# A DiT-like block on one core: V gathered per pair of tiles in five copies, attention weights transposed by DMA, rows of a pair permuted

## The chip, the core and the metric

The kernel runs on one core of a Trainium2 chip. Such a core has five engines with their own instruction streams: TensorE (PE; its weight loads are listed apart, as PEld), VectorE (DVE), ScalarE (ACT), GpSimd (POOL) and SyncE (SP). Sixteen DMA engines move data; SP and ACT issue the transfers. The engines wait for each other by semaphores only. The metric is the device time of one execution, in microseconds. A profile is one execution, recorded; its durations are given in us or ns.

## The reference

One block with adaptive layer norms: x is 2048 tokens by 512, the attention has 32 heads of 16 and looks at 8 earlier tokens with a step of 2, the FFN has width 1792.

```python
mod = (_silu(c) @ w_mod).reshape(c.shape[0], 6, 1, -1)
sa, ca, ga, sb, cb, gb = ...
h = _layernorm(x) * (1 + ca) + sa
x = x + ga * _A_ref(h, A_wqkv, A_wo)
h = _layernorm(x) * (1 + cb) + sb
x = x + gb * _B_ref(h, B_w1, B_w3, B_w2)
# _A_ref: 32 heads, Dh = 16, W = 8, dil = 2
idx = pos[:, None] - off[None, :]            # off = 0, 2, ... 14; masked where idx < 0
logits = einsum('bhsd,bhswd->bhsw', q, k[idx]) * Dh ** -0.5
o = einsum('bhsw,bhswd->bhsd', softmax(logits), v[idx])   # then @ wo
# _B_ref: (silu(h @ w1) * (h @ w3)) @ w2
```

## The kernel before, in words

The 2048 tokens are 16 tiles T of 128. Work is recorded as operations, each with its engine, and emitted in the fixed list `ORDER`; `SLOTS` says which buffer or PSUM bank each value takes. So each engine's order is written out, and an engine that waits for one operation holds up all that stand behind it. Waits are worked out from the data and the buffers.

Loads: x comes in six copies (`load_x`, L412), then `w_mod` in parts, wqkv, and the other weights, all issued by SP in the order of the list; only c is issued by ACT. All loads of SP share one queue.

Modulation: PE multiplies `w_mod` by the activated c (L504, L487 for scale and shift; L531 for the two gates ga and gb, whose weights are the buffers `sb_wm_g`). The first gate is multiplied into wo (L946), the second into w2 (L952).

LayerNorm 1 (L555 to L576) makes normalised tiles; PE transposes (L636) or DMA transposes of `ln_T` make h with features on partitions; ACT applies scale and shift (L621, L644).

Projections (L691, L711): q and k with features on partitions, evicted by ACT (L700, L701) into q buffers and into one kT for all tokens; v with tokens on partitions, evicted by ACT (L721) into one of three V buffers and stored to a scratch tensor in DRAM.

Attention, for a pair of tiles at a time: DVE multiplies q by the 8 shifted k (L742, one instruction of 4096 columns per tile). PE sums over each head's 16 features (L752): 16 matmuls per tile, each with 32 output partitions, four of which run side by side in four column groups q. A group's 32 tokens lie in the columns, so logits stand as heads x tokens. DVE and ACT make the softmax (L764 to L797). PE transposes the weights (L807) and ACT evicts them (L811) into `sb_al`. For each tile four copies from the V scratch bring the 8 shifted V rows of 32 tokens each (`values`, L816): on a partition stand 2 neighbouring tokens of one offset, 2048 bytes. DVE multiplies V by the weights in place (L827, 4096 columns), PE sums over the 8 offsets (L855, by `ind2`), ACT evicts (L861), a DMA transposes the result (`sb_ot`), PE multiplies by wo (L867), and DVE adds to x and sums the row (L871).

FFN, in groups of two or four tiles: LayerNorm 2 (L586 to L601), transposes, then for each of 14 slices of F two groups of four matmuls (L883), silu on ACT (L889), product on DVE (L892); then w2 (L921, L909), the last addition on DVE (L931) and the store by SP. FFN matmuls of earlier groups are interleaved with the attention of later pairs.

Of the kernel before, what the change touches and what calls it, by code (L numbers as in the profile page):

```python
# [10 lines left out]
P = 128  # L11
# [62 lines left out]
class Program:  # L74
# [41 lines left out]
    def dma(self, out, in_, key, packets, r=(), w=(), part=(), after=(), eng="sp", cost=450, group=None, transpose=False,  # L116
            store=False, again=False, lat=None):
# [11 lines left out]
        o = self.op(eng, fn, cost, key, r=r, w=w, part=part, after=after, dma=(each, ns, *(lat if lat else (900, 200) if store else (900, 500) if transpose else (1300, 600))))  # L129
        if group is not None:  # L130
            group.append(o)
            o.group = group
        return o
# [115 lines left out]
C_PQ, C_RED, C_ACC = 2203, 455, 800  # L249
# [3 lines left out]
def c_mm(n):  # L253
    return n * 5 // 12 + 3

# [13 lines left out]
AC_OLD = ()  # L269
# [3 lines left out]
def _build(p, A_x, A_wqkv, A_wo, B_w1, B_w3, B_w2, c, w_mod, out):  # L273
# [4 lines left out]
    x_view = x2d.rearrange("(t p) d -> p t d", p=P)  # L278
# [11 lines left out]
    qb = [sb([P, KT, 512], bf, f"q{i}") for i in range(4)]  # L290
# [3 lines left out]
    vshb = [sb([P, 8, D], bf, f"vsh{i}") for i in range(2)]  # L294
    pqb = [sb([P, W, KT, P], bf, f"pq{i}") for i in range(2)]
    NSM = 3
    atb = [sb([P, 2, 32, W], bf, f"attn{i}") for i in range(NSM)]
    alb = [sb([P, 2, 8, H], bf, f"al{i}") for i in range(3)]
    mxb = [sb([P, 2, 32], f32, f"mx{i}") for i in range(NSM)]
    ssb = [sb([P, 2, 32], f32, f"ssum{i}") for i in range(NSM)]  # L300
    otb = [sb([P, KT, P], bf, f"ot{i}") for i in range(3)]
# [5 lines left out]
    ones = sb([P, 256], bf, "ones")  # L307
    ind = sb([P, 16], bf, "ind")
    ind2 = sb([P, 2, 32], bf, "ind2")
    before = sb([P, W, 2, 16], bf, "before")  # L310
# [26 lines left out]
    osb = [nc.alloc_sbuf_tensor_at(f"sb_o{i}", [P, D], bf, offset=nc.lookup_mloc(wqkv).addr + 8192 + 1024 * i) for i in range(4)]  # L337
    vsh_x = nc.alloc_sbuf_tensor_at("sb_vshx", [P, 8, D], bf, offset=nc.lookup_mloc(wqkv).addr)
# [12 lines left out]
    vshpool = Pool("vsh", vshb)  # L351
    pqpool = Pool("pq", pqb)
# [8 lines left out]
    def held(pool, items):  # L361

        vals = []
        for i, item in enumerate(items):
# [5 lines left out]
    qkv_hold = held(vshpool, [vsh_x]) + held(opool, osb)  # L370

    vind2 = Val("ind2")
# [16 lines left out]
                                           pattern=[[-W, 16]], channel_multiplier=1), 200, k, w=[vind])  # L389
    p.op("pool", lambda e: e.affine_select(out=ind[:], in_=ind[:], compare_op=ALU.is_ge, fill=0.0, base=W - 1,  # L390
                                           pattern=[[W, 16]], channel_multiplier=-1), 200, k, w=[vind])
    p.op("dve", lambda e: e.memset(ind2[:], 0.0), 80, k, w=[vind2])
    for y in range(2):
        p.op("dve", lambda e, y=y: e.tensor_copy(bass.AP(ind2, 33 * y, [[64, P], [2, 16]]), ind[:]), 150, k, r=[vind], w=[vind2])
    p.op("pool", lambda e: e.memset(before[:], 0.0), 250, k, w=[vbefore])
    p.op("pool", lambda e: e.affine_select(out=before[:], in_=before[:], compare_op=ALU.is_ge, fill=BEFORE, base=0,
                                           pattern=[[-DIL, W], [1, 2], [2, 16]], channel_multiplier=0), 400, k, w=[vbefore])
# [14 lines left out]
    def load_x(a, b, i):  # L412
        p.dma(x_sb[:, a:b, :], x_view[:, a:b, :], ("load", i), (128 * (b - a), 1024), w=vx[a:b])
# [99 lines left out]
    def warm(i, after=()):  # L513
# [3 lines left out]
        def mm(e):  # L517
            return e.matmul(bank(vw)[:, 0:256], ones[:, 0:P], ones[:], start=True, stop=True)
# [156 lines left out]
    def proj_qk(gi, Ts, kind, vh):  # L675
# [7 lines left out]
        for f0 in range(0, KT, m):  # L683
# [13 lines left out]
            def ev(e, f0=f0, vp=vp):  # L697
                src = bank(vp)[:, 0:m * n].rearrange("p (j n) -> p j n", j=m)
                if kind == 0:
                    return e.activation(dstv.at[:, f0:f0 + m, at0:at0 + n], src, ACT.Copy, scale=SCALE)  # L700
                return e.activation(kT[:, f0:f0 + m, PAD + 512 * cch + at0:PAD + 512 * cch + at0 + n], src, ACT.Copy)  # L701
# [3 lines left out]
    def proj_v(T, tt, vh):  # L705
# [19 lines left out]
        p.dma(v_dram[PAD + T * P:PAD + (T + 1) * P, :], lambda: vt.at[:], k, (128, 1024), r=[vt], w=[vd], cost=400, store=True)  # L725
# [5 lines left out]
    def logits(Ts):  # L731

        vl = Val("ps_l", psum)
        for i, T in enumerate(Ts):
# [11 lines left out]
            def red(e, i=i, T=T, vp=vp):  # L746
                c0 = vl.at * 512 + i * W * 32
                if T == 0:
                    e.matmul(PALL[0:32, c0:c0 + W * 32], ones[:, 0:32], before[:], start=True, stop=False, tile_position=(0, 0))
                for ft in range(KT):  # L750
                    for q in range(4):
                        ins = e.matmul(PALL[32 * q:32 * q + 32, c0:c0 + W * 32], E_sb[:, ft, :], bass.AP(vp.at, ft * P + 32 * q, [[W * KT * P, P], [KT * P, W], [1, 2], [2, 16]]),  # L752
                                       start=(ft == 0 and (T > 0 or q > 0)), stop=(ft == KT - 1), tile_position=(0, 32 * q))
# [3 lines left out]
        return vl  # L757

    def shift(Ts, vl):
# [4 lines left out]
        o = p.op("dve", lambda e: e.tensor_reduce(ve.at[1][:, 0:n], bass.AP(PALL, bank(vl).offset, [[8 * 512, P], [W * 32, n], [1, 32], [32, W]]),  # L764
                                                  AX.X, ALU.max), 66 + 267 * n, k, r=[vl], w=[vm], hold=[ve], lock=False)

        def sub(e):
            l = bank(vl)[:, 0:n * W * 32].rearrange("p (n w t) -> p n w t", n=n, w=W)
            return e.tensor_tensor(l, l, bass.AP(ve.at[1], 0, [[64, P], [32, n], [0, W], [1, 32]]), ALU.subtract)
# [5 lines left out]
    def exps(groups, vls, ves):  # L775
# [3 lines left out]
        def ex(e):  # L779
            for Ts, vl in zip(groups, vls):  # L780
                l = bank(vl)[:, 0:len(Ts) * W * 32]
                ins = e.activation(l, l, ACT.Exp)
# [6 lines left out]
    def softmax(Ts, vl, ve, vx_):  # L789
# [4 lines left out]
        o = p.op("dve", lambda e: e.tensor_reduce(ve.at[2][:, 0:n], bass.AP(PALL, bank(vl).offset, [[8 * 512, P], [W * 32, n], [1, 32], [32, W]]),  # L794
                                                  AX.X, ALU.add), 66 + 267 * n, k, r=[vx_], w=[vs], hold=[ve, vl], lock=False)
        o = p.op("dve", lambda e: e.reciprocal(ve.at[2][:, 0:n], ve.at[2][:, 0:n]), 20 + 225 * n, k, r=[vs], w=[vr], hold=[ve, vl], lead=o, lock=False)
        p.op("dve", lambda e: e.tensor_tensor(ve.at[0][:, 0:n], bass.AP(PALL, bank(vl).offset, [[8 * 512, P], [W * 32, n], [1, 32], [32, W]]),  # L797
                                              bass.AP(ve.at[2], 0, [[64, P], [32, n], [1, 32], [0, W]]), ALU.mult),
             74 + 267 * n, k, r=[vr, vx_], w=[va], hold=[ve, vl], lead=o, lock=False)
        vt, val = Val("ps_at", psum), Val("al", alpool)  # L800

        def turn(e):
            b = bank(vt).bitcast(bf)
            for i in range(n):
                at = b[:, i * 256:(i + 1) * 256].rearrange("p (q y h) -> p q y h", q=4, y=2)
                for y in range(2):
                    ins = e.transpose(at[:, :, y, :], bass.AP(ve.at[0], i * W * 32 + y * 16 * W, [[2 * W * 32, P], [1, P]]), ident[:])  # L807
# [3 lines left out]
        p.op("act", lambda e: e.activation(val.at[:, 0:n].rearrange("p n g h -> p (n g h)"), bank(vt).bitcast(bf)[:, 0:2 * n * P], ACT.Copy),  # L811
# [3 lines left out]
    def values(T, i, val):  # L815

        vv = Val("vsh", vshpool)
        loads = []
        for q in range(4):
            p.dma(lambda q=q: vv.at[:, 2 * q:2 * q + 2, :],  # L820
                  bass.AP(v_dram, (PAD + T * P + 32 * q) * D, [[2 * D, 16], [-DIL * D, W], [1, 2 * D]]), ("vl", T), (128, 2048),
                  r=[vv_dram[T]] + ([vv_dram[T - 1]] if T else [vvpad]), part=[vv], group=loads, cost=640, again=True)

        def av(e):
            a_w = bass.AP(val.at, i * 8 * H, [[2 * 8 * H, P], [H, 8], [0, DH], [1, H]])
            v_w = bass.AP(vv.at, 0, [[8 * D, P], [D, 8], [H, DH], [1, H]])
            return e.tensor_tensor(v_w, v_w, a_w, ALU.mult)  # L827

        avs[T] = p.op("dve", av, C_PQ, ("av", T), r=[val], w=[vv], lock=True)
        vo = Val("ps_o", psum)  # L830

        vt = Val("ot", otpool)
        if T in AC_OLD:
            def acc(e):
                b = bank(vo)
                for g in range(8):
                    for ft in range(KT):
# [238 lines left out]
```

## Time and profile before

| what | value |
|---|---|
| median of 3 runs | 243.87 us (242.85 to 245.49) |
| profiled execution, own time | 242.82 us |
| its span in the profile | 241.1 us |
| granted PE clock | 1.00 throughout |
| DMA moved | 38.85 MB, mean 161 GB/s |
| V gathers | 64 copies of 256 KB, 4.3 to 4.6 us from issue to landing |
| V stores | 16 copies of 128 KB, 5.9 us |
| output stores | 14 of 128 KB, 1.9 us; 4 of 64 KB, 1.5 us |
| DMA transposes | 20 for h (3.9 us), 16 for `sb_ot` (3.3 us) |

How to read the page: busy time of each engine with its share of the span; then DMA queues; then the chain of work that ended last, followed back from the last instruction; then groups of instructions, as "line engine operation out<-in xcount". Busy PE time counts the modelled end of pipelined matmuls, so the number of columns says more about PE's work than its busy time: in the chain, 27 matmuls of 512 columns take 5.99 us. Busy shares of the DMA engines can be over 100%, where an engine has two packets under way. The profile's slices of 6 us show how work is spread (busy tenths; DMA the mean of its 16 engines):

```profile
PE   7988999979999999999799999999999999999995
DVE  5697999979989999898999999764565044423542
ACT  2296497688999744955964578646537253140300
DMA  6999999999979996693893882253220300000103
```

### The profile page before, as it was taken

What the parts mean: (1) busy time and instruction counts of PE and PEld (TensorE: products, weight loads), DVE (VectorE), ACT (ScalarE), POOL (GpSimd) and SP (SyncE); (2) the same over time, 40 slices, a digit from 0 to 9 for tenths busy, and PEclk for the clock granted to TensorE, in tenths of its full rate; (3) what the DMA queues carried; (4) which work ended last, traced back from release to release, by engine and by line L of the source; (5) the groups of instructions that cost most, each with busy time, mean ns of one, the idle gap of its engine ahead of it and who ended that gap; (6) DMA issues with size and microseconds to landing.
All of it is one profiled execution on the core that took longest, in us unless ns stands there. A gap on an engine that the chain in (4) does not pass through costs nothing.

```text
span 241.1 us, 4538 instructions
## 1 busy us (share of the span) xinstructions
PE 230.4 (96%) x1781; PEld 136.8 (57%) x1806; DVE 179.6 (75%) x279; ACT 138.7 (58%) x267; POOL 30.9 (13%) x66
## 2 busy tenths in 40 slices
PE   7988999979999999999799999999999999999995
PEld 4856454544587685564345444444565584485874
DVE  5697999979989999898999999764565044423542
ACT  2296497688999744955964578646537253140300
POOL 4332060004001000250005301001001000000000
PEclk9999999999999999999999999999999999999999
DMA  6999999999979996693893882253220300000103
GB/s 222 370 327 327 163 262 234 287 282 343 331 134 253 283 270 115 160 272 99 213 256 119 195 197 46 66 141 98 76 79 0 46 0 0 3 22 0 48 0 109
DMA packets 46317, 38.85 MB, mean 161 GB/s; under 512 B 21704, under 2 KB 37080, under 8 KB 46296
## 3 DMA queue, kind: packets, MB, share of 16 engines
q1 hardware_dynamic: 46288, 38.56, 62.5%
q8 instruction: 14, 0.23, 0.4%
q14 instruction: 7, 0.06, 0.1%
q10 hardware_dynamic: 8, 0.00, 0.0%
HBM read 29.62 MB, written 4.21 MB: 140 GB/s over the span
## 4 chain that ended last, share of the span: by engine, by line
PE 50%; ACT 1%; DMA 1%; issue 1%; DVE 0%; SPq 0%
PE pall L883 30%; PE pall L921 12%; PE pall L867 3%; PE pall L909 3%; DMA sb_h<-sb_xn 1%; ACT sb_h L621 1%; PE pall L855 1%; PE pall L752 1%; PE pall L807 0%; ACT sb_al L811 0%; DVE sb_o L931 0%; SPq L124 0%
## 5 line engine op out<-in xcount | busy, mean ns | idle before, releaser
L883 PE MATMUL pall<-sb_h,sb_w 128*128 128x256 bf16 (+1 forms) x665 | 101.8, 307 | 1.0 <-ACT sb_h L621 0.6
L883 PEld LDWEIGHTS pall<-sb_h,sb_w 128*128 128x128 bf16 x672 | 64.8, 98 | 36.2 <-issue 1.5
L892 DVE TENSOR_TENSOR sb_hh<-sb_sg,pall 128x256 bf16<-128x256 bf16 (+1 forms) x84 | 40.4, 505 | 32.1 <-PE pall L883 32.0
L889 ACT ACTIVATE sb_sg<-pall 128x256 bf16<-128x256 f32 (+1 forms) x84 | 36.2, 455 | 43.4 <-PE pall L883 37.3
L921 PE MATMUL pall<-sb_w,sb_hh 128*128 128x512 bf16 x189 | 43.7, 379 | 0.4
L742 DVE TENSOR_TENSOR sb_pq<-sb_q,sb_kT 128x4096 bf16<-128x4096 bf16 x16 | 36.3, 2282 | 0.0
L921 PEld LDWEIGHTS pall<-sb_w,sb_hh 128*128 128x128 bf16 x196 | 19.1, 98 | 21.0
L691 PE MATMUL pall<-sb_h,sb_wqkv 128*128 128x512 bf16 (+1 forms) x159 | 30.3, 336 | 0.1
L827 DVE TENSOR_TENSOR sb_vsh<-sb_vsh,sb_al 128x4096 bf16<-128x4096 bf16 x12 | 27.3, 2286 | 2.4 <-ACT sb_al L811 2.2
L621 ACT ACTIVATE sb_h<-sb_h,sb_modc 128x512 bf16<-128x512 bf16 (+1 forms) x24 | 16.3, 733 | 13.0 <-DMA sb_h<-sb_xn 13.0
L691 PEld LDWEIGHTS pall<-sb_h,sb_wqkv 128*128 128x128 bf16 x160 | 15.1, 98 | 12.2 <-ACT sb_h L644 0.5
L931 DVE TENSOR_TENSOR sb_o<-pall,sb_x 128x512 bf16<-128x512 f32 (+1 forms) x18 | 10.9, 627 | 11.8 <-PE pall L921 8.7
L586 POOL TENSOR_SCALAR sb_nm<-sb_sx 128x2 f32<-128x2 f32 x8 | 3.7, 465 | 115.9 <-DVE sb_x L871 115.9
L590 ACT ACTIVATE sb_xn<-sb_x,sb_nm 128x512 bf16<-128x512 bf16 x16 | 11.4, 714 | 11.7 <-POOL sb_nm L586 11.7
L867 PE MATMUL pall<-sb_wo,sb_ot 128*128 128x512 bf16 x60 | 15.0, 379 | 1.1 <-DMA sb_ot<-sb_ac 0.5
L711 PE MATMUL pall<-sb_wqkv,sb_h 128*128 128x512 bf16 x58 | 15.0, 379 | 0.3 <-issue 0.2
L644 ACT ACTIVATE sb_h<-pall,sb_modc 128x256 bf16<-128x256 bf16 (+1 forms) x18 | 9.9, 616 | 8.6 <-DVE sb_modc L509 6.7
L601 ACT ACTIVATE sb_xn<-sb_x,sb_nb,sb_rs 128x512 bf16<-128x512 bf16 x16 | 12.6, 806 | 3.7 <-POOL sb_nb L599 3.7
L871 DVE SCALAR_TENSOR_TENSOR sb_x<-pall,sb_x 128x512 bf16<-128x512 f32 x16 | 11.0, 688 | 2.3 <-PE pall L867 2.3
L701 ACT ACTIVATE sb_kT<-pall 128x512 bf16<-128x512 f32 x16 | 9.6, 606 | 4.7 <-PE pall L691 4.7
L555 DVE BATCH_NORM_STATS2 sb_st<-sb_x 128x6 f32<-128x512 bf16 x16 | 10.4, 678 | 1.3 <-DMA sb_x<-in_A_x_dram 1.3
L721 ACT ACTIVATE sb_v<-pall 128x512 bf16<-128x512 f32 x16 | 9.6, 612 | 2.4 <-DMA v_scratch_dram<-sb_v 2.3
(87 smaller groups left out, 208.6 us busy)
## 6 DMA issues: line engine op xcount, KB each, us to landing
sb_vsh<-v_scratch_dram SPq DMA_DIRECT2D x48, 256.0 KB, 4.6
sb_vshx<-v_scratch_dram SPq DMA_DIRECT2D x16, 256.0 KB, 4.3
sb_w<-in_B_w_dram SPq DMA_DIRECT2D x6, 512.0 KB, 5.6
sb_w<-in_B_w_dram SPq DMA_DIRECT2D x6, 384.0 KB, 6.0
v_scratch_dram<-sb_v SPq DMA_DIRECT2D x16, 128.0 KB, 5.9
out_dram<-sb_o SPq DMA_DIRECT2D x14, 128.0 KB, 1.9
sb_wqkv<-in_A_wqkv_dram SPq DMA_DIRECT2D x6, 256.0 KB, 6.0
sb_x<-in_A_x_dram SPq DMA_DIRECT2D x4, 256.0 KB, 6.3
```

The costliest lines, as they stand in the source:

```text
L590: p.op("act", lambda e, vn=vn, T=T: e.activation(vn.at[:], x_sb[:, T, :], ACT.Square, bias=nm[:, T, :], accum_out=var[:, T, :]), c_act(512 ...
L601: p.op("act", lambda e, vn=vn, T=T: e.activation(vn.at[:], x_sb[:, T, :], ACT.Identity, bias=nb[:, T, :], scale=rs[:, NT + T, :]), c_act(5 ...
L621: return e.activation(vh.at[:, ft, 0:n * P], vh.at[:, ft, 0:n * P], ACT.Identity, bias=modc[:, 8 * which + ft:8 * which + ft + 1], scale=m ...
L691: ins = e.matmul(bank(vp)[:, j * n:(j + 1) * n], wqkv[:, t, col:col + P], vh.at[:, t, 0:n], start=(t == ORDER[0] and j == 0), stop=(t == O ...
L711: ins = e.matmul(bank(vp), vh.at[:, t, tt * P:(tt + 1) * P], wqkv[:, t, 2 * D:3 * D], start=(t == ORDER[0]), stop=(t == ORDER[-1]))
L742: return e.tensor_tensor(vp.at[:], in0, in1, ALU.mult)
L827: return e.tensor_tensor(v_w, v_w, a_w, ALU.mult)
L867: ins = e.matmul(bank(vy), vt.at[:, ft, :], wo[:, ft, :], start=(ft == 0), stop=(ft == KT - 1))
L883: ins = e.matmul(bank(vp)[:, 0:n], wt[:, t, fi * P:(fi + 1) * P], vh.at[:, t, 0:n], start=(t == 0), stop=(t == KT - 1))
L889: p.op("act", lambda e: e.activation(vt.at[:, 0:n], bank(vgp)[:, 0:n], ACT.Silu), c_act(n), k, r=[vgp], w=[vt], table="silu")
L892: p.op("dve", lambda e: e.tensor_tensor(vh_.at[:, 0:n], vt.at[:, 0:n], bank(vup)[:, 0:n], ALU.mult), c_dve(n), k, r=[vt, vup], w=[vh_])
L921: ins = e.matmul(bank(vz), vhh[fi].at[:, tt * P:(tt + 1) * P], w2[:, fi, :], start=(fi == 0), stop=(fi == NF - 1))
```

## The change

What it does:

- **V.** The unit is a pair of tiles, 256 tokens, as 32 blocks of 8 tokens. A partition of the gathered V holds one block and one of 4 offsets (steps of 4 tokens); ten tokens' rows lie on it, brought by 5 copies of 256 KB per pair (before: 4 per tile, 8 per pair). DVE multiplies them in three instructions (6, 2 and 8 rows of 512 columns), partly into a new buffer `sb_av`; PE sums by `ind` (32 columns).
- **Attention weights** are transposed by a DMA issued by SP instead of by PE with an ACT eviction. `AT_PE` is empty, so it is so for all pairs.
- **Rows of a pair are permuted**: tile T's partition p = 32 q + b holds token 8 b + 4 (T mod 2) + q of the pair. x loads, V stores and output stores pick the rows by their DRAM pattern. The q and k evictions write back in the tokens' natural order (a step of 8 elements), and the matmuls that sum over a head's features read with that step.
- **x** is loaded in 16 copies, tile by tile, the second issued by ACT.
- Three q buffers instead of four, two `sb_ot` buffers of a pair instead of three of a tile; six output buffers instead of four.
- `ORDER` and `SLOTS` are new. The gate weights are loaded behind all of x; the second gate's matmuls come first of the two, still ahead of most of the projections.

```diff
+    def rows(t, T, c0=0, n=D):
+        first = T // 2 * 2 * P + T % 2 * 4
+        return bass.AP(t.tensor, t.offset + first * D + c0, [[D, 4], [8 * D, 32], [1, n]])
...
+    def v_rows(T):
+        return bass.AP(v_dram, (PAD + T // 2 * 2 * P + T % 2 * 4) * D, [[D, 4], [8 * D, 32], [1, D]])
...
     def load_x(a, b, i):
-        p.dma(x_sb[:, a:b, :], x_view[:, a:b, :], ("load", i), (128 * (b - a), 1024), w=vx[a:b])
+        for T in range(a, b):
+            p.dma(x_sb[:, T, :], rows(x2d, T), ("load", i if T == a else 40 + T), (128, 1024), w=[vx[T]], eng="act" if T == 1 else "sp")
...
             def ev(e, f0=f0, vp=vp):
-                src = bank(vp)[:, 0:m * n].rearrange("p (j n) -> p j n", j=m)
+                src = bass.AP(PALL, bank(vp).offset, [[8 * 512, P], [256, 2], [32, 8], [1, 32]])
...
+                    out_ = bass.AP(dstv.at, f0 * 512 + at0, [[KT * 512, P], [step_, 2], [1, 8], [8, 32]])
+                    return e.activation(out_, src, ACT.Copy, scale=SCALE)
...
-        p.dma(v_dram[PAD + T * P:PAD + (T + 1) * P, :], lambda: vt.at[:], k, (128, 1024), r=[vt], w=[vd], cost=400, store=True)
+        p.dma(v_rows(T), lambda: vt.at[:], k, (128, 1024), r=[vt], w=[vd], cost=400, store=True)
...
                     for q in range(4):
-                        ins = e.matmul(PALL[32 * q:32 * q + 32, c0:c0 + W * 32], E_sb[:, ft, :], bass.AP(vp.at, ft * P + 32 * q, [[W * KT * P, P], [KT * P, W], [1, 2], [2, 16]]),
-                                       start=(ft == 0 and (T > 0 or q > 0)), stop=(ft == KT - 1), tile_position=(0, 32 * q))
+                        ins = e.matmul(group(q), E_sb[:, ft, :], bass.AP(vp.at, ft * P + q, [[W * KT * P, P], [KT * P, W], [4, 2], [8, 16]]),
+                                       start=(ft == 0), stop=(ft == KT - 1), tile_position=(0, 32 * q))
...
+        if Ts[0] not in AT_PE:
+            p.dma(lambda: val.at[:], lambda: ve.at[0][:], ("at", Ts[0]), (128, 1024), r=[va], w=[val], hold=[ve], cost=1270, transpose=True)
+            return val
...
-        for q in range(4):
-            p.dma(lambda q=q: vv.at[:, 2 * q:2 * q + 2, :],
-                  bass.AP(v_dram, (PAD + T * P + 32 * q) * D, [[2 * D, 16], [-DIL * D, W], [1, 2 * D]]), ("vl", T), (128, 2048),
+        for s in range(5):
+            p.dma(lambda s=s: vv.at[:, 2 * s:2 * s + 2, :],
+                  bass.AP(v_dram, (PAD + T0 * P - DIL + 2 * s) * D, [[8 * D, 32], [-2 * DIL * D, 4], [1, 2 * D]]), ("vl", T0), (128, 2048),
...
+        first = p.op("dve", av(1, 2, 6, 2, vpr, 0), c_av(6), k, r=[val, vin], w=[vhigh], hold=[vv, vpr], lock=True)
+        p.op("dve", av(1, 0, 2, 0, vv, 0), c_av(2), k, r=[val, vin], part=[vlow], hold=[vv], lock=True)
+        o = p.op("dve", av(0, 0, 8, 2, vv, 2), c_av(8), k, r=[val, vin], part=[vlow], hold=[vv, vpr], lock=True)
...
-        finals.append(p.dma(out2d[T * P:(T + 1) * P, c0:c0 + n], lambda: vo.at[:, 0:n], ("zo", T), (128, 2 * n), r=[vo], cost=400, store=True))
+        finals.append(p.dma(rows(out2d, T, c0, n), lambda: vo.at[:, 0:n], ("zo", T), (128, 2 * n), r=[vo], cost=400, store=True))
```

More of the change, by code (lines that the diff above doesn't have):

```diff
@@ L128, in dma @@
         ns = 600 if transpose else each * (126 if again else packet_ns(size))
-        o = self.op(eng, fn, cost, key, r=r, w=w, part=part, after=after, dma=(each, ns, *(lat if lat else (900, 200) if store else (900, 500) if transpose else (1300, 600))))
+        o = self.op(eng, fn, cost, key, r=r, w=w, part=part, after=after, hold=hold, dma=(each, ns, *(lat if lat else (900, 200) if store else (900, 500) if transpose else (1300, 600))))
         if group is not None:
@@ L248 @@
 MM = 216
[L249 removed]
+C_PQ, C_RED = 2203, 455
 BEFORE = -1e9 / P
@@ L863, in values @@
-        vy = Val("ps_y", psum)
-        def wop(e):
-            for ft in range(KT):
-                ins = e.matmul(bank(vy), vt.at[:, ft, :], wo[:, ft, :], start=(ft == 0), stop=(ft == KT - 1))
-            return ins
-        p.op("pe", wop, 4 * MM, ("wo", T), r=[vt, vsc_wo], w=[vy])
-        p.op("dve", lambda e: e.scalar_tensor_tensor(x_sb[:, T, :], bank(vy), 1.0, x_sb[:, T, :], op0=ALU.mult, op1=ALU.add,
-                                                     accum_out=sx[:, T, :]), c_dve(512) + 12, ("rs", T), r=[vy], w=[vx[T], vsx[T]])
+        for s in range(5):
+            p.dma(lambda s=s: vv.at[:, 2 * s:2 * s + 2, :],
+                  bass.AP(v_dram, (PAD + T0 * P - DIL + 2 * s) * D, [[8 * D, 32], [-2 * DIL * D, 4], [1, 2 * D]]), ("vl", T0), (128, 2048),
+                  r=[vv_dram[T] for T in Ts] + ([vv_dram[T0 - 1]] if T0 else [vvpad]), part=[vin], hold=[vv], group=loads, cost=640, again=True)
@@ new lines, in values, with wop @@
+        for n, T in enumerate(Ts):
+            vy = Val("ps_y", psum)
+            def wop(e, n=n, vy=vy):
+                for ft in range(KT):
+                    ins = e.matmul(bank(vy), vt.at[:, ft, n * P:(n + 1) * P], wo[:, ft, :], start=(ft == 0), stop=(ft == KT - 1))
+                return ins
+            p.op("pe", wop, 4 * MM, ("wo", T), r=[vts[n], vsc_wo], w=[vy], hold=[vt])
+            p.op("dve", lambda e, T=T, vy=vy: e.scalar_tensor_tensor(x_sb[:, T, :], bank(vy), 1.0, x_sb[:, T, :], op0=ALU.mult, op1=ALU.add,
+                                                         accum_out=sx[:, T, :]), c_dve(512) + 12, ("rs", T), r=[vy], w=[vx[T], vsx[T]])
```

169 lines of the change are left out of this document (83 added, 86 removed), and 126 rows, old and new, of tables (ORDER, SLOTS).

## The prediction, made before the changed kernel ran

> **What bounds the kernel now.** I read the page first, then the chain that ended last, TensorE's waits, its timeline, and last the DMA traffic in narrow windows. The page's engine and queue rows (engine or queue: busy us, share, instructions; for queues packets, MB, share of 16 engines):
>
> ```profile
> span 241.1 us, 4538 instructions
> PE 230.4 (96%) x1781; PEld 136.8 (57%) x1806; DVE 179.6 (75%) x279; ACT 138.7 (58%) x267; POOL 30.9 (13%) x66
> q1 hardware_dynamic: 46288, 38.56, 62.5%
> q10 hardware_dynamic: 8, 0.00, 0.0%
> ```
>
> TensorE (PE) is the bound, DVE is second, and DMA is far from full over the whole span. The chain in order of time (start, duration, what) says where PE is the bound:
>
> ```profile
> 116.50 5.99 PE pall L883 x27
> ...
> 232.34 6.13 PE pall L909 x56
> 238.47 0.02 issue
> 238.49 0.42 DVE sb_o L931
> ```
>
> From 116.5 us on every piece but waits of some 0.05 us is PE work; then the last eviction, and the last store to 241.1 (2.6 us after PE). Before that, PE waited for data in few places (total, times, longest):
>
> ```profile
> PE pall L531 <- DMA sb_wm_g<-in_w_mod_dram: 1.5, 2, 0.9
> PE pall L752 <- ACT sb_kT L701: 0.9, 1, 0.9
> PE pall L855 <- DVE sb_vsh L827: 0.7, 1, 0.7
> ```
>
> All rows of PE's list of waits sum to about 7 us. The first matters here: the matmuls on the gate weights wait for their load. They stand early in PE's order (timeline: start, duration):
>
> ```profile
> 18.10 0.54 PE L531 MATMUL pall<-sb_csT_bf,sb_wm_g 128*128 128x1 bf16 x16 [0.63 <-DMA sb_wm_g<-in_w_mod_dram]
> ```
>
> Now DMA. In the window 4 to 16 us the 16 engines are full, so a load lands when the bytes ahead of it are through:
>
> ```profile
> DMA packets 3595, 4.42 MB, mean 369 GB/s; under 512 B 191, under 2 KB 2693, under 8 KB 3594
> q1 hardware_dynamic: 3594, 4.41, 107.2%
> ```
>
> That is 369/16 = 23.1 GB/s per engine. How many engines one copy uses can be counted. The window 239.3 to 241.1 holds the last store alone, 128 rows of 512 B:
>
> ```profile
> DMA packets 144, 0.07 MB, mean 36 GB/s; under 512 B 16, under 2 KB 144, under 8 KB 144
> ```
>
> 128 rows make 128 packets, and 16 more are small: one completion from each of 16 engines. The load of c, four rows of 256 B on queue 10, has 8 packets: four rows and four completions, so four engines. By the code, the access patterns of all other copies begin on both sides with a count of 128, 32 or 16, those of c with 4.
>
> **The change, part by part.** Times are against the profiled execution: 242.82 us, span 241.1, so 1.7 us lie around the span; it is 0.4% under the median of 243.87.
>
> 1. *Attention weights by DMA.* Removes 8 groups of 4 PE transposes (L807): 0.22 us each when hidden in the chain, so 8 x 0.22 = -1.8 us on PE, on the path; and 8 ACT evictions (L811, 598 ns) = -4.8 us, off it. The DMA takes the place of at most 2.4 us (the first pair's weights are ready at 36.3, their first user starts at 38.7); the like DMA, sb_ot<-sb_ac, lands in 3.3 us, behind an SP issue of 1.3. In the new DVE order 3.5 to 17 us of other DVE work by its rows stand between the weights and their first user, so DVE waits 0 to 1 us per pair, and the matmuls of L691 and L883 lie beside it. I take 0 on the path, ends 0 and 8.
>
> 2. *V copied 5 instead of 8 times.* 64 copies of 256 KB become 40: -24 x 16 KB per engine = -17 us per DMA engine at 23.1 GB/s, off the path. SP issues 24 fewer at 0.6 us, 8 more transposes at 1.3 and 9 more x loads at 0.45: -14.4 + 10.4 + 4.1, so nothing.
>
> 3. *DVE.* The two products of a pair (2286 ns each) become three over the same 8192 columns. L952 (2048 columns 1219 ns, 1536 columns 950 ns) gives 0.14 us fixed per instruction: 8 x 0.14 = +1.1 us, beside L883 matmuls; 0 on the path. The softmax rows keep their sizes. Two small copies (L394) go, at the start, beside ACT's table load: 0.
>
> 4. *Rows of a pair permuted, inside the chip.* Matmuls of L752 read their moving operand with a step of 8 elements (now 2), and the q and k evictions (L700, L701) write with that step. No row shows such a step. Nearest: L752 itself at full speed (32 in 0.99 us), and L721, which reads PSUM with a step of 16 at 612 ns against 606 without. I take 0; the bounds are no cost, or half speed: 16 tiles x 0.495 us = +7.9 us on PE.
>
> 5. *Start.* A second DMA issue on ACT (0.56 us) now precedes its table load, which leads by way of c to the first LayerNorm: +0.5 us, on the path unless 6 covers it.
>
> 6. *Rows of a pair permuted, in DRAM.* This is the large term. The x loads, the V stores and the output stores now have on the DRAM side the counts 4, 32, 512: they begin with 4. By the count above I take it that such a copy runs on four engines, and that these are the same four each time (the trace cannot show which; the bound if they rotate is a rival). Then in queue order, ahead of the end of the first gate load, each of those four engines has x 2.10 MB / 4 = 524 KB, the modulation weights 1.05 MB / 16 = 66 KB, wqkv 98 KB, the gate load 33 KB: 721 KB / 23.1 = 31.2 us. Bytes begin at about 2.3 us, so it lands at 33.5, with 0.5 us to its completion 34.0, against 18.1 now. In the new PE order the gate matmuls still stand before the transposes of the third LayerNorm group and nearly all else. PE is in order, so what is queued behind them waits: all remaining projections, attention and FFN. That is +15.9 us. Earlier waits are inside it (96 KB more of x stand ahead of wqkv, 4.2 us). Nothing late in the kernel can take it back: PE ran from 18.10 to 238.47 with 4 us of waits.
>
>    V stores: 128 KB / 4 / 23.1 = 1.42 us each on the four engines instead of 0.36: 16 x 1.06 = +17 us of their time, against 12 x 0.71 = -8.5 us for the gathers saved in the first four pairs. Three V buffers stand between ACT and the stores; ACT already waits for a store three times (2.3 us in all). Behind a waiting V eviction on ACT stand the q and k evictions, which hold PSUM banks, so PE waits too. Bounds 0 and 17; I take +5, nearer the difference of the two with half of it hidden.
>
>    Output stores: only the last one is on the path: 64 KB, 16 KB per engine at 23.1 GB/s = 0.7 against 0.2: +0.5 us.
>
> Sum: 242.8 - 1.8 + 15.9 + 5 + 0.5 = 262.4; the 0.5 of part 5 lies inside the 15.9.
>
> [...]
>
> **The rivals.**
>
> *A, four fixed engines:* 262. For: the eight packets of queue 10. Against: those four rows could not have used more than four engines anyway.
>
> *B, faster:* the copies still use 16 engines. Then PE's own wall decides: 242.8 - 1.8 + 0.5 = 241.5, and the new order can at most remove the waits, 5 us: 236.5 to 241.5, so 239.5. For: PE's share of the chain. It decides where an x load shows 16 completions.
>
> *C, as B, but strided reads halve L752:* 239.5 + 7.9 = 247.4. For: the step is new. Against: a step of 2 costs nothing in L752. [...]
>
> *D, four engines that rotate:* no queue grows, each copy takes 1.1 us longer: first x load +1.1, last store +0.5, two waits for V stores +2: 239.5 + 3.6 = 243. The "does little" case.
>
> **How the numbers follow.** Chances: A 0.72, B 0.12, C 0.08, D 0.08. The forecast is A's 262. A's own range: with no cost of V stores and 3.4 us of the remaining waits gone, 254; with 17 instead of 5 for V stores, 274: so 254 to 274. To leave out no more than 2 in 10 the range must take in C and D: 242 to 276 (A inside 0.66, C 0.08, D 0.06, a little of B). About 1% is what a measurement of this kernel can tell from no change: 241.4 to 246.3. Faster by over 1% is B, 0.12; within 1% is D and the fastest edge of A, 0.09; slower is the rest of A, and C, 0.79.
>
> **What would show it.** Right: an x load window with 128 rows and 4 small packets; x loads that land near 20 to 33 us; PE waiting over 10 us for sb_wm_g; the DMA share well under full at 10 to 35 us, with GB/s falling to about a quarter; more ACT waits at the V eviction. Part 1 is right if L807 is gone and DVE waits little for sb_al. C is right if the L752 group's 32 take near 2 us. Wrong: 16 small packets per x load, or a PE wait for the gates under 3 us; then B or C holds. If the four engines rotate, x loads land within 20 us although each has 4 completions.

## The result, and the profile after

| kernel | median, us | ratio to before, 95% interval |
|---|---|---|
| before | 243.8 (242.85 to 245.49) | |
| changed | 315.4 (314.47 to 315.7) | 1.2921 [1.2844, 1.2997] |

The change costs 29%, 71.6 us, far beyond the forecast of 262 and its upper end of 276. Some executions take over 1.5% longer than the fastest of the same kernel; they stay in the medians here and are left out of the ratios. The page of the changed kernel (engines, then queues):

```profile
span 314.0 us, 4468 instructions
PE 265.0 (84%) x1752; PEld 139.7 (44%) x1777; DVE 180.4 (57%) x284; ACT 190.6 (61%) x259; POOL 28.9 (9%) x69
q1 hardware_dynamic: 46612, 33.19, 41.3%
q10 hardware_dynamic: 140, 0.13, 0.1%
```

DMA moves 5.4 MB less on queue 1, as the five V copies should. But PE, at 96% of the span before, is at 84%, and although its matmul work hardly changed it is busy 34.6 us longer. ACT is busy 51.9 us longer with eight instructions fewer. Queue 10 carries c (8 packets) and one x load: 132 packets, which are 128 rows and 4 completions. The slices of the span (here 7.85 us each, busy tenths; PEclk the granted clock) say where:

```profile
PE   6693199756897568998989999999999999999990
ACT  2189858989999997975483662457356543421300
PEclk9997569977799797999999999999999999999997
DMA  6625999760146650792465323532232202100012
```

PE has holes up to 120 us (slice 15) and a last slice with nothing. ACT is full in most of the slices in which PE has holes, and where PE starves its granted clock is lower, too: 5 tenths in slice 5, where PE is busy 1 tenth. The groups (line, engine, operation, tiles, forms, count, then busy us, mean ns, and the idle time before) name the instructions. Before, the q and k evictions and the reduction matmuls were

```profile
L701 ACT ACTIVATE sb_kT<-pall 128x512 bf16<-128x512 f32 x16 | 9.6, 606 | 4.7 <-PE pall L691 4.7
L700 ACT ACTIVATE sb_q<-pall 128x512 bf16<-128x512 f32 x16 | 9.3, 606 | 0.0
L752 PE MATMUL pall<-sb_pq,sb_E 128*32 128x256 bf16 x256 | 9.1, 271 | 0.9 <-ACT sb_kT L701 0.9
```

and in the changed kernel they are

```profile
L714 ACT ACTIVATE sb_q<-pall 128x512 bf16<-128x512 f32 x16 | 40.5, 2596 | 2.7 <-PE pall L703 2.7
L716 ACT ACTIVATE sb_kT<-pall 128x512 bf16<-128x512 f32 x16 | 41.5, 2629 | 0.7 <-PE pall L703 0.6
L770 PE MATMUL pall<-sb_pq,sb_E 128*32 128x256 bf16 x256 | 31.4, 631 | 1.2 <-ACT sb_kT L716 0.8 <-DVE sb_pq L757 0.4
```

An eviction took 606 ns and now takes 2.6 us: +63 us by these rows, whose durations overlap their neighbours' (ACT's busy time grew by 51.9). The 256 reduction matmuls took 9.1 us and now take 31.4: +22 us on PE. Both gained the step of 8 elements. The gate matmuls (timeline: start, duration, and in brackets the wait) start at 37.8 instead of 18.1:

```profile
37.84 0.57 PE L543 MATMUL pall<-sb_csT_bf,sb_wm_g 128*128 128x1 bf16 x16 [7.62 <-DMA sb_wm_g<-in_w_mod_dram]
```

At the end PE's last matmuls (timeline: start, duration) are

```profile
299.56 6.28 PE L926 MATMUL pall<-sb_w,sb_hh 128*128 128x256 bf16 x56
```

They end at 305.8 us, and the last store lands at 314.0: 8.1 us behind PE, where there were 2.6. (The chain that ended last leaves PE earlier, at 301.3 us, since the last evictions wait for output buffers and no longer for PE. So 12.7 us of the chain lie behind it. The texts written ahead of the runs take these 12.7 us for the time behind PE's last instruction.) DMA traffic in the window 308 to 311 us, with only output stores under way:

```profile
DMA packets 339, 0.28 MB, mean 92 GB/s; under 512 B 10, under 2 KB 339, under 8 KB 339
```

92 GB/s is four times the 23.1 GB/s of one engine (369/16 before), and queue 1 takes 27.5% of the 16 engines' time there: by rate and share the stores queue on the same four engines while twelve are empty. The list of waits (total us, times, longest) shows the new ones:

```profile
DVE sb_pq L757 <- ACT sb_q L714: 17.9, 1, 17.9
PE pall L543 <- DMA sb_wm_g<-in_w_mod_dram: 7.8, 2, 7.6
DVE sb_o L948 <- DMA out_dram<-sb_o: 7.6, 4, 4.4
```

So three suspects: the DRAM pattern that begins with 4 (start and tail), ACT's writes with a step of 8 (to SBUF, where the buffers lie; PSUM holds the banks that PE writes), PE's reads with a step of 8. What each is worth, how they overlap, and whether anything is left of the rest of the change, the trace alone can't say.

### The profile page after: what moved, and what is told of

Its sections match the earlier page's. It is cut to its first block, busy times and chain, and to the rows that moved or that the text cites. A ratio compares the mean times of both kernels' runs of the same rounds, so it can differ in the third digit from the quotient of the medians.

```text
span 314.0 us, 4468 instructions
## 1 busy us (share of the span) xinstructions
PE 265.0 (84%) x1752; PEld 139.7 (44%) x1777; DVE 180.4 (57%) x284; ACT 190.6 (61%) x259; POOL 28.9 (9%) x69
## 2 busy tenths in 40 slices
DMA packets 46773, 33.61 MB, mean 107 GB/s; under 512 B 25232, under 2 KB 40608, under 8 KB 46752
## 4 chain that ended last, share of the span: by engine, by line
PE 60%; ACT 20%; SPq 9%; DMA 6%; issue 2%; DVE 0%; ACTq 0%; DVEq 0%
PE pall L900 30%; PE pall L938 13%; SPq L124 9%; ACT sb_q L714 8%; PE pall L770 7%; ACT sb_kT L716 7%; DMA sb_wm_g<-in_w_mod_dram 4%; PE pall L884 4%; ACT sb_h L633 2%; PE pall L871 2%; PE pall L703 2%; PE pall L726 2%; DMA out_dram<-sb_o 1%; DMA sb_ot<-sb_ac 1%; ACT sb_v L736 1%
## 5 line engine op out<-in xcount | busy, mean ns | idle before, releaser
L906 ACT ACTIVATE sb_sg<-pall 128x256 bf16<-128x256 f32 (+1 forms) x84 | 36.4, 463 | 44.7 <-PE pall L900 37.6
L703 PE MATMUL pall<-sb_h,sb_wqkv 128*128 128x512 bf16 (+1 forms) x155 | 36.5, 379 | 12.7 <-ACT sb_q L714 7.4
L714 ACT ACTIVATE sb_q<-pall 128x512 bf16<-128x512 f32 x16 | 40.5, 2596 | 2.7 <-PE pall L703 2.7
L716 ACT ACTIVATE sb_kT<-pall 128x512 bf16<-128x512 f32 x16 | 41.5, 2629 | 0.7 <-PE pall L703 0.6
L770 PE MATMUL pall<-sb_pq,sb_E 128*32 128x256 bf16 x256 | 31.4, 631 | 1.2 <-ACT sb_kT L716 0.8
L938 PEld LDWEIGHTS pall<-sb_w,sb_hh 128*128 128x128 bf16 x196 | 19.1, 98 | 21.4
L851 DVE TENSOR_TENSOR sb_vsh<-sb_vsh,sb_al 128x1024 bf16<-128x1024 bf16 (+1 forms) x16 | 23.3, 1484 | 0.1
L656 ACT ACTIVATE sb_h<-pall,sb_modc 128x256 bf16<-128x256 bf16 (+1 forms) x18 | 10.6, 657 | 14.0 <-DVE sb_modc L521 11.0
L726 PE MATMUL pall<-sb_wqkv,sb_h 128*128 128x512 bf16 x60 | 17.5, 426 | 1.8 <-ACT sb_q L714 0.8
L876 ACT ACTIVATE sb_ac<-pall 128x512 bf16<-128x512 f32 x16 | 9.8, 639 | 15.2 <-PE pall L871 11.9
L598 POOL TENSOR_SCALAR sb_nm<-sb_sx 128x2 f32<-128x2 f32 x8 | 2.4, 298 | 160.6 <-DVE sb_x L888 160.6
```

What stands on the lines that cost most here:

```text
L703: ins = e.matmul(bank(vp)[:, j * n:(j + 1) * n], wqkv[:, t, col:col + P], vh.at[:, t, 0:n], start=(t == ORDER[0] and j == 0), stop=(t == O ...
L714: return e.activation(out_, src, ACT.Copy, scale=SCALE)
L716: return e.activation(out_, src, ACT.Copy)
L726: ins = e.matmul(bank(vp), vh.at[:, t, tt * P:(tt + 1) * P], wqkv[:, t, 2 * D:3 * D], start=(t == ORDER[0]), stop=(t == ORDER[-1]))
L770: ins = e.matmul(group(q), E_sb[:, ft, :], bass.AP(vp.at, ft * P + q, [[W * KT * P, P], [KT * P, W], [4, 2], [8, 16]]), start=(ft == 0), s ...
L906: p.op("act", lambda e: e.activation(vt.at[:, 0:n], bank(vgp)[:, 0:n], ACT.Silu), c_act(n), k, r=[vgp], w=[vt], table="silu")
```

## The experiments

Each suspect was first taken out of the changed kernel alone, then all three together; then each was put back alone; then the disputed costs were measured by themselves. Medians of four or more executions, beside runs of the kernel before on the same chip:

| run | what is in it | median, us | ratio to before, 95% interval |
|---|---|---|---|
| changed | DRAM 4 x 32, writes, reads | 315.4 | 1.2921 [1.2844, 1.2997] |
| e1_rows | writes, reads | 303.92 | 1.2491 [1.2447, 1.2536] |
| e2_evict | DRAM, reads | 286.85 | 1.1806 [1.1773, 1.1838] |
| e3_red | DRAM, writes | 303.35 | 1.2486 [1.2448, 1.2524] |
| e4_all | none of the three | 243.45 | 1.0025 [0.9989, 1.006] |
| f1_dram | DRAM alone | 270.14 | 1.1092 [1.1034, 1.1149] |
| f2_write | writes alone | 290.85 | 1.1968 [1.1924, 1.2013] |
| f3_read | reads alone | 261.57 | 1.0786 [1.0743, 1.083] |

### One suspect out

**e1_rows**: 128 rows side by side in DRAM.

```
-        first = T // 2 * 2 * P + T % 2 * 4
-        return bass.AP(t.tensor, t.offset + first * D + c0, [[D, 4], [8 * D, 32], [1, n]])
+        return bass.AP(t.tensor, t.offset + T * P * D + c0, [[D, P], [1, n]])
...
-        return bass.AP(v_dram, (PAD + T // 2 * 2 * P + T % 2 * 4) * D, [[D, 4], [8 * D, 32], [1, D]])
+        return bass.AP(v_dram, (PAD + T * P) * D, [[D, P], [1, D]])
```

> The changed kernel with one edit: the x loads, the V stores and the output stores take 128 rows that lie next to each other in DRAM (counts 128, 512) instead of 4 x 32 rows (counts 4, 32, 512); the same number of DMAs and bytes. What is computed is then not the reference: tokens meet other tokens' keys. Theory (the four-first pattern puts each of these DMAs on the same four engines): each such DMA shows 16 completion packets, the gate load lands at about 18 us as before instead of 37.8, the work behind PE's last instruction falls from 12.7 us to about 3, and the time falls by 10 us (the tail alone, if ACT's evictions go on bounding the middle) to 26 us (tail and the 15.9 us of the start as forecast): 288 to 304. Rival (the evictions and the reduction matmuls carry all of the loss): 312 to 316.

303.92 us, 11.5 less, at the low end of what was expected. The packet rows of its page:

```profile
DMA packets 47373, 33.61 MB, mean 111 GB/s; under 512 B 25832, under 2 KB 41208, under 8 KB 47352
q10 hardware_dynamic: 152, 0.13, 0.1%
```

Against 46,773 packets in the changed kernel that is 600 more: 50 copies (16 x, 16 V, 18 outputs) with 12 completions more each, so 16 instead of 4. That a completion stands for an engine is an inference. The rates of the changed kernel agree with it: several stores together move 92 GB/s in the tail, and with x loads alone under way (18 to 24 us) DMA moves 96 GB/s at 27.2% of the 16 engines' time, which is what the same four engines would do each time; no run here shows their numbers. About half of the 11.5 us is the tail: 8.1 us behind PE's last matmul became 2.5. Of the start little is left: the gate matmuls begin 12.9 us earlier (24.9 instead of 37.8), but the last k eviction only 6.9 us earlier (132.6 instead of 139.5), as ACT is full between 20 and 120 us with or without late x loads (93.1 and 93.6 of 100 us).

**e2_evict**: the step goes to the PSUM side.

```
-                src = bass.AP(PALL, bank(vp).offset, [[8 * 512, P], [256, 2], [32, 8], [1, 32]])
+                src = bass.AP(PALL, bank(vp).offset, [[8 * 512, P], [256, 2], [1, 32], [32, 8]])
...
-                    out_ = bass.AP(dstv.at, f0 * 512 + at0, [[KT * 512, P], [step_, 2], [1, 8], [8, 32]])
+                    out_ = bass.AP(dstv.at, f0 * 512 + at0, [[KT * 512, P], [step_, 2], [8, 32], [1, 8]])
```

> The changed kernel with one edit: the q and k evictions read PSUM with a step of 32 elements and write 8 tokens side by side, where they read side by side and wrote with a step of 8 elements (16 bytes); same result in SBUF. Theory (the step of the write makes them 2.6 us): L714 and L716 go back to about 0.61 us each, ACT's busy time falls by 63 us to about 128 us, PE's granted clock stays at 1.00 from 60 to 120 us, and the time falls by 15 to 36 us (PE is idle 36 us of 301): 278 to 299. Rival (any step costs the same on either side, in PSUM as in SBUF): L714 and L716 stay above 2 us and the time at 312 to 318.

286.85 us, 28.5 less. The groups of its page:

```profile
L716 ACT ACTIVATE sb_kT<-pall 128x512 bf16<-128x512 f32 x16 | 9.5, 604 | 1.7 <-PE pall L703 1.6
L714 ACT ACTIVATE sb_q<-pall 128x512 bf16<-128x512 f32 x16 | 9.4, 601 | 12.8 <-PE pall L703 12.7
```

The same elements, moved to the same places, at the old price: reading PSUM with a step of 32 elements costs nothing here (604 and 601 ns, where both took 606 before), writing SBUF with a step of 8 costs 2 us (2629 and 2596 ns in the changed kernel). ACT's busy time fell by 55 us, to 135.3, and not by the 63 of the rows that overlap. This edit alone would have saved two fifths of the loss.

**e3_red**: `[4, 2], [8, 16]` plus `q` becomes `[1, 2], [2, 16]` plus `32 * q` in the moving operand of L770.

> The changed kernel with one edit: the reduction matmuls L770 read the products with a step of 2 elements (4 bytes) as in the kernel before, not 8 elements (16 bytes); their PSUM pattern with runs of 16 elements stays. The logits then go to other tokens, so that what is computed is not the reference. Theory (the read's step makes 16 of them 1.9 us): L770 falls from 31.4 us to about 9 us of PE, and the time by up to 22 us, by less where ACT's evictions are what PE waits for: 292 to 312. Rival (the runs of 16 in PSUM, or the four column groups that no longer run side by side for the new output pattern): L770 stays at about 31 us and the time at 314.

303.35 us, 12.1 less, within the theory's range. The group of L770, whose PSUM pattern stayed:

```profile
L770 PE MATMUL pall<-sb_pq,sb_E 128*32 128x256 bf16 x256 | 10.5, 298 | 0.8 <-ACT sb_kT L716 0.8
```

So it is the read's step, not the new runs in PSUM. (The 10.5 instead of 9.1 us come from some of the matmuls: half of them take at most 271 ns, as before, and the slowest 418, in a run whose granted clock was 0.92 on average.)

**e4_all**: the three edits together.

> The three edits together (rows side by side in DRAM, evictions that write 8 tokens side by side, reduction reads with a step of 2): what is left is the rest of the change, V in 5 copies, weights turned by DMA, the new order. What is computed is not the reference, for the same two reasons as in the runs alone. Theory (the three explain the whole loss): 238 to 246, ACT about 128 us, L770 about 9 us. Rival (the new order or the DMA-turned weights cost by themselves): over 250, with DVE or PE waiting for the turned weights or the V copies.

243.45 us, no difference from before that can be measured. The page:

```profile
span 240.9 us, 4493 instructions
PE 230.8 (96%) x1777; PEld 134.6 (56%) x1777; DVE 179.3 (74%) x284; ACT 135.1 (56%) x259; POOL 31.0 (13%) x69
```

The three carry the whole loss, and the rest of the change (V in five copies, weights turned by DMA, the new order) is worth nothing: 5 MB less DMA beside a PE at 96%.

### One suspect in

**f1_dram**, **f2_write** and **f3_read** are e4_all with one of its edits undone.

> The run with all three edits, with the DRAM pattern of four times 32 rows put back: of the three suspected costs only this one is left. The logits go to other tokens (reduction reads with a step of 2), so what is computed is not the reference. Theory (start and tail each cost their own, and nothing hides them): the gate load lands near 38 us, PE is idle some 12 us between 20 and 40 us, 12 to 13 us lie behind PE's last instruction, and the time is 262 to 270, the prediction's own 262 among it. Rival (costs add up as they were when each was taken away alone, 11.5 us for this one): 253 to 257.

270.14 us, +26.7, just above the theory's upper end. Its chain over 27 to 41 us (start, duration, what) holds the gate load:

```profile
26.58 1.25 SPq L124
27.83 0.04 issue
27.87 11.35 DMA sb_wm_g<-in_w_mod_dram
39.22 0.14 issue
39.36 0.57 PE pall L543 x16
```

SP is held at its issues until 27.8 us (12 x loads in a row take it 18.4 us, in e4_all 5.8), and the gate load then takes 11.4 us; that it lies behind what is left of x on the four engines is inferred from the order of the queue. At the end 8.1 us lie behind PE's last matmul (2.5 in e4_all), not the 12 to 13 expected.

> The run with all three edits, with the eviction writes of step 8 put back: only they are left. Rows in DRAM are side by side and the logits go to other tokens, so what is computed is not the reference. Theory (ACT becomes the bound from 20 to 120 us, as L714 and L716 take 2.6 us each): ACT's busy time about 190 us, its slices full from 20 to 110 us, the time 270 to 285. Rival (the writes only hurt because the late x loads had pushed all of ACT's work together): under 260.

290.85 us, +47.4, more than either expected. Busy times between 20 and 120 us (window, length, PE, PEld, DVE, ACT, POOL, granted clock, DMA share, GB/s), f2_write:

```profile
20.00:120.00 100.00, 66.80 (x472) 29.90 (x481) 50.63 (x65) 95.35 (x87) 4.98 (x12) 0.83 0.47 125
```

and e4_all:

```profile
20.00:120.00 100.00, 95.89 (x845) 55.46 (x843) 95.69 (x130) 74.44 (x140) 15.82 (x23) 1.00 0.83 203
```

ACT is full, does 87 instead of 140 instructions, and PE does 472 instead of 845 matmuls in the same time. Of ACT's extra 55 us (190.1 against 135.1), the 25.6 us in which e4_all's ACT is idle here could hide less than half. PE's 66.8 us at a mean clock of 0.83 are, as an estimate, 55 us of work at full speed, 40 us less than in e4_all, and PE has to make that up later: most of the 47.4. The last k eviction begins at 130.0 us instead of 82.2, so the whole loss has arisen by then.

> The run with all three edits, with the reduction reads of step 8 put back: only they are left. Rows in DRAM are side by side and the tokens of a tile meet other tokens' keys, so what is computed is not the reference. Theory (PE is the bound at 96% of the span, so every us of L770 counts): L770 31 us, the time 243.5 + 22 = 262 to 268. Rival (costs add up as they were when each was taken away alone, 12 us for this one): 253 to 257.

261.57 us, +18.1, just below the theory's 262. PE is busy 250.0 us of 259.9, 19.2 us more than in e4_all: where PE is the bound, its dearer matmuls are the loss.

Put in alone, the three cost 26.7 + 47.4 + 18.1 = 92.2 us; together 315.4 - 243.45 = 72.0. DRAM and writes together (e3_red) cost 59.9 instead of 74.1, writes and reads (e1_rows) 60.5 instead of 65.5, DRAM and reads (e2_evict) 43.4, about their sum of 44.8. So 14 of the 20 us of overlap lie between late x and slow ACT, which hold up the same early stretch (late x delays the last k eviction by 22.8 us alone, 105.0 against 82.2, and by 6.9 beside the slow writes), and 5 between ACT and the matmuls that wait for it.

### The costs by themselves

**m1_steps**: e4_all with other steps; the warm-up matmul, for one of six cases:

```
-            return e.matmul(bank(vw)[:, 0:256], ones[:], bass.AP(ones, 0, [[P, P], [0, 2], [1, P]]), start=True, stop=True)
+            if i % 6 == 3:
+                return e.matmul(o, ones[:], bass.AP(ones, 0, [[P, P], [0, 16], [8, 16]]), start=True, stop=True)
```

> The run with all three edits, with steps of other sizes to measure the disputed cost by itself. The 24 warm-up matmuls (full width, 256 columns, about 214 ns, which nothing uses) read with steps of 1, 2, 4, 8, 16 and 32 elements in turn; the reduction matmuls read with a step of 4, PSUM written in runs of two with a step; q is written with a step of 4 elements, k with a step of 2, in orders that send tokens elsewhere (what is computed is not the reference). Theory (the read's rate falls with the step above 4 bytes): warm-up matmuls with steps of 8 and more take 3 to 5 times as long as those with step 1, a step of 4 lies between, and L770 takes 9 to 20 us. Rival (a step alone costs nothing; the four column groups of L770 stopped running side by side): all warm-up matmuls take the same time within 10%. For the writes, theory: a cost that grows with the step: k (step 2, 4 bytes) about 0.6 us, q (step 4, 8 bytes) between 0.6 and 2.6 us.

255.75 us in one execution, which has other steps in three places at once; only its instructions matter. The timeline, where the six lines have the steps 1, 2, 4, 8, 16 and 32 (start, then the modelled duration; the next start gives the time of one):

```profile
5.62 0.39 PE L531 MATMUL pall<-sb_ones 128*128 128x256 bf16 x1
5.81 0.42 PE L533 MATMUL pall<-sb_ones 128*128 128x256 bf16 x1
6.03 0.41 PE L535 MATMUL pall<-sb_ones 128*128 128x256 bf16 x1
6.26 0.63 PE L537 MATMUL pall<-sb_ones 128*128 128x256 bf16 x1
6.71 0.64 PE L539 MATMUL pall<-sb_ones 128*128 128x256 bf16 x1
7.17 0.61 PE L540 MATMUL pall<-sb_ones 128*128 128x256 bf16 x1
```

From start to start 0.19, 0.22 and 0.23 us up to a step of 4, then 0.45, 0.46 and (to 7.60) 0.43: a step of 8 doubles it, and no larger step costs more. That is a factor of two, under the three to five expected, but these early matmuls take 0.19 us even with no step (256 columns take 0.11 at the end of the changed kernel, 56 matmuls in 6.28 us) and so may hide a smaller cost. And the groups:

```profile
L724 ACT ACTIVATE sb_q<-pall 128x512 bf16<-128x512 f32 x16 | 21.0, 1346 | 2.9 <-PE pall L713 2.9
L780 PE MATMUL pall<-sb_pq,sb_E 128*32 128x256 bf16 x256 | 16.8, 406 | 0.1
L726 ACT ACTIVATE sb_kT<-pall 128x512 bf16<-128x512 f32 x16 | 12.7, 805 | 0.7 <-PE pall L713 0.6
```

A set of four reduction matmuls, one for each column group, takes 9.1 / 64 = 0.14 us with a step of 2, 0.26 with 4 (where runs of two in PSUM are new as well; the two weren't told apart) and 0.49 with 8. The four together take hardly longer than one warm-up matmul of step 8 (0.45), where four in a row would take 1.8: the column groups still run side by side. And the warm-up matmuls, which have no column groups, slow down with the step, too: the rival is out. An eviction takes 600 ns with no step, 805 with 2, 1346 with 4, 2.6 us with 8: 1.3, 1.7 and 1.9 times as long for each doubling.

**h1_x, h2_v, h3_out**: e4_all with the 4 x 32 pattern in one kind of copy alone, for instance

```
-            p.dma(x_sb[:, T, :], rows(x2d, T), ...
+            p.dma(x_sb[:, T, :], rows(x2d, T, four=True), ...
```

> The run with all three edits, with the DRAM pattern of four times 32 rows put back in the 16 x loads alone. Rows that are then mixed with the others' order make the output other than the reference. Theory (late x loads and the gate load behind them leave PE idle at the start): the gate load lands at 34 to 40 us, little lies behind PE's last instruction (about 3 us), and the time is 256 to 262, that is 13 to 18 us of the 27 that the pattern costs in all three places. Rival (the start is made up later, since PE finds work in another order): under 248.

261.51 us, ratio 1.0731 [1.0663, 1.0798], +18.1, within the theory's range; the gate matmuls start at 37.6 us. Windows 20 to 30 and 30 to 40 us, columns as above:

```profile
20.00:30.00 10.00, 5.03 (x37) 3.50 (x34) 6.13 (x17) 3.54 (x8) 2.96 (x7) 0.83 0.33 113
30.00:40.00 10.00, 2.70 (x48) 2.16 (x47) 1.70 (x7) 2.12 (x4) 0.94 (x3) 0.50 0.94 250
```

PE idles over 12 of these 20 us, at first with DMA at a third of its capacity, and its clock falls to half.

> The run with all three edits, with the DRAM pattern of four times 32 rows put back in the 16 V stores alone; tokens are mixed up as in the run before. Theory (a store of 128 KB on four engines lands some 4 us after its issue, but V is read late enough): 243 to 248, as the prediction's 5 us at most. Rival (the V copies wait for the stores, and with them the multiplications on DVE): 250 or more, with DVE waiting for the copies.

247.97 us (244.01 to 248.81). The four executions spread too far for a ratio: the two lowest, 244.01 and 247.45 us, lie 0.6 and 4.0 us above e4_all's median, whose own executions reach from 242.64 to 247.28, so a cost of nothing is not excluded. ACT's waits for V stores sum to 1.4 us, and DVE waits for no V copy, so the rival is out.

> The run with all three edits, with the DRAM pattern of four times 32 rows put back in the output stores alone; tokens are mixed up as before. Theory (the last stores queue behind each other on the same four engines): nine stores land one after another, about 12.7 us lie behind PE's last instruction instead of about 3, and the time is 252 to 255. Rival (the prediction's 0.5 us: only the last store is slower): 243 to 245.

250.11 us, ratio 1.0271 [1.0212, 1.0329], +6.7: between the two theories. The last nine stores, 5 x 128 KB and 4 x 64 KB, are 0.92 MB; at four engines' 92 GB/s they need 10 us. The kernel's end shifts by less, since the first of them start while PE still works and 2.5 us were behind PE anyway: 8.0 us lie behind PE's last matmul, 5.5 more than in e4_all. The rest is a PE that ends 1.9 us later in the profiled execution (240.2 against 238.4 us); no run shows that the stores cause it.

**g1_split**: the changed kernel with e2_evict's evictions, reduction reads with a step of 4 (`[8, 16], [4, 2]`), and each x load, V store and output store cut in four.

```
-        return bass.AP(t.tensor, t.offset + first * D + c0, [[D, 4], [8 * D, 32], [1, n]])
+        return [bass.AP(t.tensor, t.offset + (first + q) * D + c0, [[8 * D, 32], [1, n]]) for q in range(4)]
```

> The changed kernel, computing the reference, with each of the three costs lowered as far as its layout allows: evictions that write 8 tokens side by side; reduction reads with a step of 4 elements (PSUM written in runs of two with a step); each x load, V store and output store cut into four DMAs of 32 rows each, 144 more DMAs. Theory: L770's line 16 to 17 us (7.6 more than with a step of 2), 16 engines for each store, the time 250 to 256 if SP's issues keep up. Rival (SP becomes the bound at the start, as 64 issues of 0.5 us or more for x take over 32 us): the gate load lands after 38 us and the time is 262 or more.

285.48 us, ratio 1.1735 [1.1677, 1.1792]: the rival. SP's timeline (start, duration, copies):

```profile
10.04 23.34 SPq L126 DMA_DIRECT2D sb_x<-in_A_x_dram  x48
33.43 0.97 SPq L127 DMA_DIRECT2D sb_wm_g<-in_w_mod_dram  x2
```

Queue 10 shows 200 packets, which are c's 8, 128 rows and 4 x 16 completions, so the quarters do use 16 engines. But SP needs 0.49 us for each, and the gate load is issued only at 33.4 us: four engines at the start were exchanged for a queue of issues. It is so at the end, too: SP's last 36 store issues take 16.6 us, and 13.3 us lie behind PE's last matmul, more than in the changed kernel. (Cutting 50 copies in four makes 150 more DMAs, not the 144 expected.) No run of this layout came out under the kernel before, and e4_all, which has none of its costs, only equals it; so no version that beats both was found.

## Why the prediction was wrong

- **Part 4, the rows permuted inside the chip, is the step that failed.** It took 0 for the step of 8 elements without a row that shows one, with half speed of L752 (+7.9 us) as the far end. The reads alone cost 18.1 us (f3_read) and made L752 3.4 times as long, not twice. The evictions had no far end at all: they were named, set beside L721, and taken as free. Alone they cost 47.4 us (f2_write). The row L721 was the wrong neighbour: it reads PSUM with a step and writes side by side, and in e2_evict a step on that side cost nothing (601 to 604 ns, 606 before). The writes of SBUF had no row. An unknown of 32 instructions on an engine with a quarter of its time left between 20 and 120 us needed a bound such as three or four times as long, and the range would have had to hold it.
- **Part 6, four engines, was right for these copies.** It took that from a single copy of four rows. The runs show more: copies whose DRAM counts begin with 4 have 4 completions, the same copies with 128 rows side by side have 16 (e1_rows), and several of the first kind together move 92 GB/s at the end, four engines' rate; rivals B and D are out. Its term was 21.4 us for the three kinds of copy; f1_dram measured 26.7. That these are so near is in part luck, as one piece was, as far as the runs show, too large and two were too small. The start, forecast as +15.9 with the gate load at 34.0, is +18.1 with the gate matmuls at 37.6 (h1_x); the 0.5 us to a completion in the 34.0 was an estimate that no run shows apart. V stores, forecast as +5, can't be told from nothing (h2_v, 0.6 and 4.0 in its two lowest executions). The output stores were mis-sized: "only the last one is on the path", +0.5, became +6.7 (h3_out, 5.5 of it behind PE's last matmul), as nine stores queue behind each other on four engines. The sum rested on an end with 2.6 us behind PE, without asking what a four times slower store does to a queue of them.
- **Parts 1, 2, 3 and 5** sum to nothing measurable in e4_all, whose 243.45 us stand where the sum had 242.8 - 1.8 + 0.5 = 241.5. The transposes and V copies went as forecast; DVE waits 1.2 us for the turned weights in e4_all. PE's -1.8 us did not show in the time, 243.45 against 243.21 for the kernel before beside it. PE's busy time, 230.8 against 230.4, can't say why: the trace of before has 25 matmul records fewer than weight loads (1781 and 1806), that of e4_all none (1777 and 1777).
- **Rival C** was right that the strided reads cost time, with a chance of 0.08 and under half their size (7.9 for 18.1 us), and it excluded the four engines: the cases were written as alternatives, where here three costs held together. The forecast of 262 stands 8 us under f1_dram's 270, where nothing of part 4 is in the kernel, and 53 us under the result, where all of it is.

## What to carry to other kernels

The price of this permutation depended on the place: read PSUM with the step (no cost in e2_evict, 601 to 604 ns an eviction and 606 before) rather than write SBUF with it (2.6 us, 4.3 times as long), and keep the steps of moving operands small (the reduction matmuls took 9.1, 16.8 and 31.4 us with steps of 2, 4 and 8). When an access has no row in the trace, its bound is not "half speed" by habit: multiply its count by several times its present duration (here it was 3.4 and 4.3 times), ask whether the engine has that much time to spare, and let the range hold it. In DRAM, see which count a pattern begins with (4 completions with 4 here, 16 with 128), and add up all copies that queue on the engines it leaves.

## What was unexpected

- An ACT write to SBUF was slower from the smallest step on: 600, 805, 1346 and 2600 ns for 128x512 elements with steps of 1, 2, 4 and 8 (e4_all, m1_steps, changed kernel).
- A starved PE paid twice here. Its granted clock fell to 0.50 where it idled at the start (h1_x, 30 to 40 us) and to 0.83 on average where ACT held it up (f2_write, 20 to 120 us). In f2_write PE was busy 245.1 us with the matmuls that take 230.8 in e4_all.
